# Windowed attention and a SoLU layer on one core: the layer's products five tiles apart, first tiles' h in halves over three PSUM banks, weights converted in contiguous staging, one batch's value means by TensorE

## The chip, the core and the metric

The kernel runs on one core of a Trainium2 chip. A core has five engines, each with its own queue of instructions: TensorE (PE, matrix products, with PEld for its weight loads), VectorE (DVE), ScalarE (ACT), GpSimd (POOL) and SyncE (SP, which here only issues transfers). An engine executes its queue in order, and waits at an instruction until the semaphores that it names have been raised by other engines or by transfers (DMA). The metric is the device time of one execution in microseconds; the time before is the median of three executions.

## What is computed

The reference, cut to what matters:

```python
def _attn_ref(q, k, v):                      # each (4, 8, 768, 64)
    block, window = (32, 16); nb = S // block; scale = 1 / sqrt(D)
    k_sum = k.reshape(B, H, nb, block, D).max(axis=3)
    v_sum = v.reshape(B, H, nb, block, D).mean(axis=3)
    scores_l = where(|i - j| < window, scale * q @ k.T, -1e9)
    scores_s = scale * einsum('bhsd,bhnd->bhsn', q, k_sum) + log(block)
    a = softmax(concatenate([scores_l, scores_s]))
    return a @ concatenate([v, v_sum])

def _moe_ref(x, w_in, w_out, g_ln):          # x (3072, 512), w_in (512, 1024), w_out (1024, 512)
    h = x @ w_in
    solu = h * softmax(h)
    ln = (solu - mean(solu)) / sqrt(var(solu) + 1e-6) * g_ln
    return ln @ w_out
```

The attention's output, laid out by tokens, is the layer's x. The weights arrive as 64-bit floats.

## The kernel before

**Tiles.** The layer runs over 24 tiles of 128 tokens (t = 0 to 23), six in each batch. Attention runs over groups of 256 queries, each in two halves of four heads; a half of a group is one step, and there are as many steps as tiles. A step has these parts, by the names in the trace: kw gathers the keys of each 64-query window (96 keys) and the 24 block maxima (ksum); s are the scores (L498, PE); e and nm the masked scores and their extremes (L518, VectorE, eight instructions); the exponentials (L526, ScalarE, eight); z their sums' reciprocals (L531, L532) and the scaling of e (L245 on VectorE or L246 on GpSimd); t the transposed e (L552, PE) and at its copy; x the values (L590, PE); xh and xl the high and low part of x in a reduced 32-bit format, of which products run in one pass.

**The layer.** `first(t)` makes h = x w_in with 24 products of 512 columns (L616: per 128 rows of w_in and half of h, low weights, low x, and both high). Then hm is h's maximum (L623), he the exponential (L625), hz its sum's reciprocal, he = h * he / z with the sum s1 (L629), he less its mean (L636 on GpSimd or L638 on VectorE), sq its squares (L641), y the reciprocal root (L646 to L652). `turn(t)` transposes he (lt, L552) and splits it into lh and ll. `second(t)` makes o with 24 products (L681), scales by y and stores. h holds two PSUM banks in one buffer, so `first(t + 1)` waits until L629 of tile t has read it.

**The main loop** (L724 to L759) records for tile t: values and scores of coming steps, `first(t)`, turns, two pieces of w_out's conversion, `second(t - LAG)` with LAG = 3 at L741, and for batch b + 1 the block maxima and means of v.

**Weights.** Each of 16 pieces (128 x 512) is loaded as 64-bit words into raw (L297) and converted in `rounded`: the high word is scaled (L315 or L317), the low word scaled and rounded (L321 or L323), both in place in raw, so that their elements stand two words apart; the high one is shifted to staging (L326), the low one gets the sign merged (L330), and GpSimd adds both (L334). Then the high half is copied (L238 or L239) and the low half subtracted (L245 or L246); for w_out L356 and L358 do so with g_ln.

**Means of v.** Batch 0's are four products with a selector on raw rows (`mean_values_first`, L400). Those of later batches are trees of GpSimd additions (`add_rows`, L418 and L422) with a small product at the end (`mean_values`, L433). They go to vsum, and `load_v2` copies them four times into each window's vt.

**What sets the order.** The kernel records operations with costs, buffers and dependencies in `Plan`; `issue()` then places them with its own model of time, choosing among engines where an operation names several (`alt`), and writes every engine's queue. An operation marked `port` counts VectorE's contention with GpSimd. `keep_up` inserts products of zeros (L766) where PE would be idle in the first 80 us of that model. Rings of buffers (`Plan.buf`) say which earlier tile must be done with a buffer.

Of the kernel before, what the change touches and what calls it, by code (L numbers as in the profile page):

```python
# [27 lines left out]
G = 4  # L28
# [9 lines left out]
LAG = 3  # L38
NHE = 4
NEAR = 4  # L40
# [3 lines left out]
LOADS = "kqkqkqkqwwwwwwwwrrrvQV"  # L44
# [4 lines left out]
class Buf:  # L49


    def __init__(self, make, prev=None):
        self.make, self.prev, self.tile = make, prev, None
        self.ops, self.writers, self.readers, self.gone = [], {}, {}, False
# [14 lines left out]
class Plan:  # L69
# [6 lines left out]
    RATE = 360.0  # L76
# [4 lines left out]
    DEAR = {"dve": 0.7, "act": 0.3}  # L81
    HELD = 1.1
    SYNC = 0.13

    def __init__(self):
        self.ops, self.rings, self.idle = [], {}, None

    def buf(self, pool, shape, dtype, tag, bufs, name):
        ring = self.rings.setdefault(tag, [])
        slot = f"{tag}_{len(ring) % bufs}"  # L90
        b = Buf(lambda: pool.tile(shape, dtype, tag=slot, bufs=1, name=name),
                ring[-bufs] if len(ring) >= bufs else None)
        ring.append(b)
        return b

    def op(self, engine, cost, fn, r=(), w=(), nbytes=0, after=(), alt=(), port=False):
# [16 lines left out]
        for b, part in w:  # L113
            of(b.writers, part)
            of(b.readers, part)
            if b.prev is not None:
                deps.update(b.prev.ops)
                b.prev.gone = True
# [11 lines left out]
    def issue(self):  # L130
        ready, free, dma = {}, {}, 0.0
# [9 lines left out]
        def enter(o, at):  # L141
            for e in o.can:
                ready.setdefault(e, []).append((at, o))
# [4 lines left out]
        def cost(e, o, t):  # L148
            held = min(max(free.get("pool", 0.0) - t, 0.0), self.HELD) if e == "dve" and o.port else 0.0
            return o.can[e][0] * (2 if e == "pe" and t < self.COLD else 1) + held  # L150
# [23 lines left out]
        for o in self.ops:  # L174
            if not o.left:
                enter(o, 0.0)
        order = []
        while len(order) < len(self.ops):
# [5 lines left out]
            o.end = free[e] = t + cost(e, o, t)  # L184
            if o.nbytes:
# [3 lines left out]
            for u in o.users:  # L189
                u.left -= 1  # L190
                if not u.left:
                    enter(u, max(d.end for d in u.deps) + self.SYNC)
# [9 lines left out]
    def keep_up(self, at, done):  # L202


        for tag in "hxs":
            b = next((b for b in self.rings[tag] if b.ops[0] not in done), None)
            if b and (b.prev is None or all(o in done and o.end + self.SYNC < at for o in b.prev.ops)):
# [6 lines left out]
def attn_then_solu(ctx: ExitStack, tc: tile.TileContext, q, k, v, vb, w_in, w_out, g_ln, out):  # L214
# [13 lines left out]
    LO_W = ((dve, 0.6), (pool, 1.4))  # L228
    MUL_E = ((pool, 1.8), (dve, 1.07))
# [62 lines left out]
    raw, stage, wi, wo = {}, {}, {}, {}  # L292
# [7 lines left out]
    def load_w_in(c, nh):  # L300
        load_w(c * 2 + nh, w_in[c * P:(c + 1) * P, nh * 512:(nh + 1) * 512])

    def load_w_out(f, after):
        load_w(2 * NKC + f, w_out[f * P:(f + 1) * P, :], after)

    def rounded(key, st, part):
# [3 lines left out]
        to = lambda: st.ap[:, part]  # L310
        high = lambda: x.ap.rearrange("p (n t) -> p n t", t=2)[:, :, 1]
        low = lambda: x.ap.rearrange("p (n t) -> p n t", t=2)[:, :, 0]
# [3 lines left out]
            out=high().bitcast(F32), in_=high().bitcast(F32), func=AF.Copy, scale=2.0 ** -112),  # L316
            w=[(x, 1)], alt=[(dve, 0.34, lambda: nc.vector.tensor_scalar(  # L317
                out=high().bitcast(F32), in0=high().bitcast(F32), scalar1=2.0 ** -112, scalar2=None,
# [3 lines left out]
            out=low(), in_=low().bitcast(U32), func=AF.Copy, scale=2.0 ** -29), w=[(x, 0)],  # L322
            alt=[(dve, 0.34, lambda: nc.vector.tensor_scalar(  # L323
                out=low(), in0=low().bitcast(U32), scalar1=2.0 ** -29, scalar2=None, op0=ALU.mult))], port=True)

        op(dve, 0.34, lambda: nc.vector.tensor_scalar(  # L326
            out=to(), in0=high(), scalar1=3, scalar2=None, op0=ALU.logical_shift_left),
            r=[(x, 1)], w=[(st, part)], port=True)
# [3 lines left out]
            r=[(x, 1)], w=[(x, 0)])  # L332

        op(pool, 1.46, lambda: nc.gpsimd.tensor_tensor(out=to(), in0=to(), in1=low(), op=ALU.add),  # L334
           r=[(x, 0)], w=[(st, part)])
        hl = plan.buf(const, [P, 2, 512], F32R, f"w{key}", 1, f"w{key}")
        return (lambda: to().bitcast(F32)), hl

    def split_w_in(c, nh):
        if nh == 0:  # L340
            stage["in", c] = plan.buf(sb, [P, 2, 512], I32, "he", NHE, f"cv_in{c}")
        st = stage["in", c]
        w, hl = rounded(c * 2 + nh, st, nh)
        wi[c, nh] = hl
        copy(COPY_W, lambda: hl.ap[:, 0], w, r=[(st, nh)], w=[(hl, 0)], port=True)
        tt(LO_W, ALU.subtract, lambda: hl.ap[:, 1], w, lambda: hl.ap[:, 0].bitcast(F32),
           r=[(st, nh), (hl, 0)], w=[(hl, 1)])

    def split_w_out(f):
        if f % 2 == 0:  # L350
            stage["out", f // 2] = plan.buf(sb, [P, 2, 512], I32, "vrow", 2, f"cv_out{f // 2}")
        st = stage["out", f // 2]
        w, hl = rounded(2 * NKC + f, st, f % 2)
        wo[f] = hl
        gs = g_sb[:, f:f + 1]
        op(act, 0.61, lambda: nc.scalar.activation(out=hl.ap[:, 0], in_=w(), func=AF.Copy, scale=gs),  # L356
           r=[(st, f % 2), g_b], w=[(hl, 0)])
        op(dve, 0.66, lambda: nc.vector.scalar_tensor_tensor(  # L358
            out=hl.ap[:, 1], in0=w(), scalar=gs, in1=hl.ap[:, 0].bitcast(F32),
            op0=ALU.mult, op1=ALU.subtract), r=[(st, f % 2), (hl, 0), g_b], w=[(hl, 1)])  # L360
# [5 lines left out]
    def load_keys(b, p, after=()):  # L366
# [4 lines left out]
        op(sp, 0.05, lambda: nc.sync.dma_start(out=x.ap[:, i], in_=k[b, p]), w=[(x, i)], nbytes=P * SP * 4,  # L371
# [12 lines left out]
    def load_v_rows(b, i):  # L384

        rows = v[b, HALO + 2 * P * i:HALO + 2 * P * (i + 1), :].rearrange("(c p) n -> p c n", p=P)
# [415 lines left out]
```

## Time and profile before

| | us |
|---|---|
| median of 3 runs (418.41 to 419.27) | 418.68 |
| the profiled execution | 419.72 |
| its span, first to last instruction | 417.9 |
| PE busy in the span | 396.2 |
| products of zeros (L766) in it | 23.4 |
| VectorE, ScalarE, GpSimd busy | 284.1, 243.6, 124.2 |

The profile shows one execution. A row of the order of time has start, duration, engine, line, operation, output<-input, shapes, a count where like instructions were merged, and in brackets how long the engine had been idle and what ended that. A row of a group has busy time, mean ns of one instruction, and idle time ahead of it. Starts of queued instructions can be closer than their durations, since one begins while the last one drains. TensorE's clock was granted at 0.992 on average, with 0.68 between 50 and 60 us.

### The profile page before, as it was taken

The page shows a single profiled execution, that of the slowest core. Times are in us where ns is not written, and L with a number is a line of the kernel's source. Part 1 is how long each engine was busy: PE and PEld are TensorE (multiplying, and loading weights), DVE is VectorE, ACT ScalarE, POOL GpSimd, SP SyncE. Part 2 cuts the span into 40 slices and gives each one's busy share as a digit, 9 for nine tenths or more (in the row PEclk, how much of TensorE's full clock was granted, in tenths as well). Part 3 has the DMA queues.
Part 4 walks back from the last instruction along what each step waited for, and adds up shares of the span by engine and source line. Part 5 has one row for each costly group of instructions (what it writes and reads, how often), then busy time and mean ns, then how long its engine had stood idle before and what let it go on. Part 6 is the DMA issues. An engine that isn't in the chain of part 4 may idle for free.

```text
span 417.9 us, 9489 instructions
## 1 busy us (share of the span) xinstructions
PE 396.2 (95%) x3667; PEld 299.3 (72%) x3667; DVE 284.1 (68%) x841; ACT 243.6 (58%) x710; POOL 124.2 (30%) x172
## 2 busy tenths in 40 slices
PE   7999598889899999999999999999999999999996
PEld 3437376567678777777877777777777777777876
DVE  4998899996877776736876764564676567453440
ACT  4967889737556745745763673675675566332231
POOL 4676546887851101108102110110110100111010
PEclk9999879999999999999999999999999999999999
DMA  8999996428337412126134220241230000000011
GB/s 268 410 256 263 327 245 164 127 78 197 91 117 200 130 49 80 52 88 153 55 100 124 77 78 27 76 102 40 77 95 29 25 6 23 27 25 2 25 50 52
DMA packets 22929, 46.03 MB, mean 110 GB/s; under 512 B 1860, under 2 KB 8260, under 8 KB 22884
## 3 DMA queue, kind: packets, MB, share of 16 engines
q1 hardware_dynamic: 18096, 36.97, 31.4%
q10 hardware_dynamic: 4788, 8.46, 6.2%
q8 instruction: 29, 0.48, 0.5%
q14 instruction: 16, 0.13, 0.1%
HBM read 36.97 MB, written 6.29 MB: 104 GB/s over the span
## 4 chain that ended last, share of the span: by engine, by line
PE 58%; DMA 16%; DVE 15%; ACT 5%; POOL 3%; issue 1%; SPq 0%; DVEq 0%
PE h L616 26%; PE o L681 22%; DMA kraw<-in_k 4%; DMA vt<-in_v 4%; DMA raw<-in_w_out 4%; DVE hm L623 3%; DVE e L518 3%; DVE he L629 3%; ACT he L625 3%; PE x L590 3%; PE lt L552 3%; DMA st_v<-in_vb 2%; PE t L552 2%; PE s L498 2%; POOL st_v L418 2%; DMA raw<-in_w_in 2%
## 5 line engine op out<-in xcount | busy, mean ns | idle before, releaser
L616 PE MATMUL h<-w,xh 128*128 128x512 f32 x384 | 141.1, 405 | 8.2 <-DVE he L629 6.9
L681 PE MATMUL o<-w,lh 128*128 128x512 f32 (+1 forms) x400 | 142.4, 394 | 0.1
L616 PEld LDWEIGHTS h<-w,xh 128*128 128x128 f32 x384 | 72.4, 189 | 31.8 <-issue 11.0
L681 PEld LDWEIGHTS o<-w,lh 128*128 128x128 f32 x400 | 74.1, 188 | 19.0 <-issue 2.9
L681 PE MATMUL o<-w,ll 128*128 128x512 f32 (+1 forms) x200 | 77.2, 386 | 0.5 <-DVE ll L666 0.5
L616 PE MATMUL h<-w,xl 128*128 128x512 f32 x192 | 75.7, 394 | 0.0
L526 ACT ACTIVATE e<-e,nm 128x120 f32<-128x120 f32 x192 | 73.0, 384 | 1.1 <-DVE nm L518 1.1
L636 POOL TENSOR_SCALAR he<-he,nmu 128x512 f32<-128x512 f32 x27 | 23.8, 883 | 99.5 <-DVE nmu L632 99.3
L625 ACT ACTIVATE he<-h,hm 128x1024 f32<-128x1024 f32 x24 | 26.7, 1114 | 42.9 <-DVE hm L623 42.8
L238 ACT COPY at<-t 120x512 f32<-120x512 f32 x45 | 24.2, 587 | 41.5 <-PE t L552 41.4
L681 PEld LDWEIGHTS o<-w,ll 128*128 128x128 f32 x200 | 37.6, 188 | 8.0 <-DVE ll L666 0.8
L518 DVE CUSTOM_DVE_ANT_0 e<-s,mask 128x120 f32<-128x120 f32 x192 | 40.5, 275 | 2.8 <-PE s L498 2.8
L616 PEld LDWEIGHTS h<-w,xl 128*128 128x128 f32 x192 | 36.3, 189 | 6.8
L623 DVE TENSOR_REDUCE hm<-h 128x1 f32<-128x1024 f32 x24 | 29.3, 1221 | 14.9 <-PE h L616 14.9
L240 POOL COPY kw<-ksum 128x192 f32<-128x192 f32 (+1 forms) x26 | 9.4, 363 | 100.6 <-PE s L498 79.9
L641 ACT ACTIVATE sq<-he 128x1024 bf16<-128x1024 f32 x24 | 25.4, 1057 | 22.6 <-POOL he L636 20.6
L239 DVE CAST lh<-lt 128x512 fp32r<-128x512 f32 x23 | 15.8, 687 | 32.4 <-PE lt L552 27.1
L666 DVE TENSOR_TENSOR ll<-lt,lh 128x512 fp32r<-128x512 f32 x48 | 31.8, 684 | 8.5 <-ACT lh L238 8.1
L418 POOL TENSOR_TENSOR st_v<-st_v 96x512 f32<-96x512 f32 (+3 forms) x42 | 33.9, 816 | 8.8 <-DMA st_v<-in_vb 6.3
L526 ACT ACTIVATION_READ_ACCUMULATOR e<-e,nm 128x1 f32 x192 | 36.3, 189 | 0.0
L590 PEld LDWEIGHTS x<-at,vt 120*64 120x64 f32 (+1 forms) x768 | 25.4, 141 | 10.4 <-issue 5.2
L629 DVE SCALAR_TENSOR_TENSOR he<-h,hz,he 128x1024 f32<-128x1024 f32 x24 | 30.7, 1278 | 0.2
(79 smaller groups left out, 525.3 us busy)
## 6 DMA issues: line engine op xcount, KB each, us to landing
vt<-in_v SPq DMA_DIRECT2D x12, 768.0 KB, 5.8
kraw<-in_k SPq DMA_DIRECT2D x16, 400.0 KB, 7.5
out<-os ACTq DMA_DIRECT2D x23, 256.0 KB, 2.0
qt<-in_q SPq DMA_DIRECT2D x11, 512.0 KB, 4.0
st_v<-in_vb SPq DMA_DIRECT2D x12, 384.0 KB, 3.7
raw<-in_w_in SPq DMA_DIRECT2D x8, 512.0 KB, 7.1
raw<-in_w_out SPq DMA_DIRECT2D x8, 512.0 KB, 12.0
vt<-vsum ACTq DMA_DIRECT2D x11, 192.0 KB
```

What stands on the lines that cost most here:

```text
L238: by = {act: lambda: nc.scalar.copy(out=to(), in_=of()), dve: lambda: nc.vector.tensor_copy(out=to(), in_=of()), pool: lambda: nc.gpsimd.t ...
L418: op(pool, 0.15 + w * 0.0021, lambda w=w, o=o: nc.gpsimd.tensor_tensor(out=o.ap[:n, :w], in0=x.ap[:n, :w], in1=x.ap[:n, w:2 * w], op=ALU.add),
L518: nc.vector.tensor_tensor_reduce(out=e.ap[:, n, :], in0=sc.ap[:, j, (2 * i + up) * KC:(2 * i + up + 1) * KC], in1=mask[:, mi, :], scale=-S ...
L526: nc.scalar.activation(out=e.ap[:, n, :], in_=e.ap[:, n, :], func=AF.Exp, bias=nm.ap[:, n:n + 1], scale=-1.0, accum_out=z.ap[:, n:n + 1])
L590: nc.tensor.matmul(xp.ap[j * D:(j + 1) * D, i, qs], vs.ap[:k, u, cs], at.ap[:k, u % 2, n[j] + u // 2, :], start=not apart, stop=not apart ...
L616: nc.tensor.matmul(o, a.ap[:, c, ts], w.ap[:, i], start=(c == 0 and n == 0), stop=(c == NKC - 1 and n == 2))
L623: op(dve, 1.13, lambda: nc.vector.tensor_reduce(out=nm.ap, in_=h.ap, op=ALU.max, axis=AX.X, negate=True), r=[h], w=[nm])
L625: op(act, 1.09, lambda: nc.scalar.activation(out=e.ap, in_=h.ap, func=AF.Exp, bias=nm.ap, accum_out=z.ap), r=[h, nm], w=[e, z])
L629: op(dve, 1.27, lambda: nc.vector.scalar_tensor_tensor(out=e.ap, in0=h.ap, scalar=z.ap, in1=e.ap, op0=ALU.mult, op1=ALU.mult, accum_out=s1 ...
L641: op(act, 1.13, lambda: nc.scalar.activation(out=sq.ap, in_=e.ap, func=AF.Square, accum_out=ss.ap), r=[e], w=[sq, ss])
L666: op(dve, 0.6, lambda part=part, r=r: nc.vector.tensor_tensor(out=part(lo), in0=tp.ap[:, r], in1=part(hi).bitcast(F32), op=ALU.subtract), ...
L681: nc.tensor.matmul(o.ap[:, cols], a.ap[:, f, :], w.ap[:, i, cols], start=(f == 0 and n == 0), stop=(f == NFC - 1 and n == 2))
```

## The change

In the order of the code:

- **LAG 5, NHE 6, NEAR 7.** `second(t)` is recorded five tiles behind `first(t)`; six buffers hold he; values and scores of a step are joined into one PE operation from tile 7 on, before from 4.
- **h in halves.** For tiles 0, 1 and 2 (EARLY = 3), the two halves of h are buffers of their own that go round over three banks, so that half of the next tile's h has a bank while the last is read; x and o then have one bank of four. From tile 3 on, h has banks 0 and 1 and x and o alternate between 2 and 3, as before. The early tiles have maximum, exponential and product of he in two instructions each, and one more to join maxima or sums.
- **Staging.** A piece's two words are converted straight to two contiguous halves of one staging buffer, one for each piece. The add may also run on VectorE: an instruction (printed as ISA) that adds 32-bit integers as 16-bit limbs.
- **Batch 1's means by TensorE** (`mean_values_pe`, MEANS = 2): raw rows vr, loaded in three pieces, four by four products with a selector in four row groups, a copy, and four small DMAs that bring 6 rows each into vsum. GpSimd's tree for that batch and its loads are gone; batches 2 and 3 keep theirs.
- **Layouts** made on the host: q by groups, k by pairs of heads, v as whole windows, batches 0 and 1 also as rows vr, so that a partition's words of a load are contiguous. First loads come as "kqkkqk", q in two loads of two head pairs.
- **The planner's numbers**: transfers at 400 instead of 360, a lower surcharge on VectorE, contention counted without a limit and also for GpSimd.

```diff
-LAG = 3
-NHE = 4
-NEAR = 4
+LAG = 5
+NHE = 6
+EARLY = 3
+MEANS = 2
+NEAR = 7
...
-LOADS = "kqkqkqkqwwwwwwwwrrrvQV"
+LOADS = "kqkkqkwwwwwwwwrrrvQV"
...
-    RATE = 360.0
+    RATE = 400.0
...
-    DEAR = {"dve": 0.7, "act": 0.3}
-    HELD = 1.1
+    DEAR = {"dve": 0.3, "act": 0.3}
...
+    ADD_W = ((dve, 0.62), (pool, 1.46))
...
-    def rounded(key, st, part):
+    def rounded(key, tag, bufs):
...
+        st = plan.buf(sb, [P, 2, 512], I32, tag, bufs, f"cv{key}")
+        words = lambda i: x.ap.rearrange("p (n t) -> p n t", t=2)[:, :, i]
+        high, low = (lambda: st.ap[:, 0]), (lambda: st.ap[:, 1])
...
-        op(pool, 1.46, lambda: nc.gpsimd.tensor_tensor(out=to(), in0=to(), in1=low(), op=ALU.add),
-           r=[(x, 0)], w=[(st, part)])
+        tt(ADD_W, ALU.add, high, high, low, r=[(st, 1)], w=[(st, 0)], port=True)
...
+    banks = ps.tile([P, 4, 512], F32, name="banks")
+    turn_x = [2]
+
+    def place_h(t, half):
+
+        if half is None:
+            return plan.place(lambda: banks[:, :2].rearrange("p i n -> p (i n)"), (0, 1), "h")
+        i = (2 * t + half) % 3
+        return plan.place(lambda: banks[:, i], (i,), "h")
+
+    def place_x(t):
+        i = 3 if t < EARLY else turn_x[0]
+        turn_x[0] = 5 - i
+        return plan.place(lambda: banks[:, i], (i,), "x")
...
+    def mean_values_pe(b):
+
+        vsum[b] = y = plan.buf(sb, [P, DM], F32, "vsum", 1, f"vsum{b}")
+        acc = plan.buf(ps, [P, 2, DM], F32, "s", 2, f"vs_ps{b}")
+        to = lambda: acc.ap[:, 0]
+
+        def mm(x, i, g, s):
+            nc.tensor.matmul(to()[g * 32:(g + 1) * 32], sel_q.ap[:, s, :], x.ap[:, i, :], start=s == 0, stop=s > 0)
...
+        rows = plan.buf(sb, [P, DM], F32, "os", 2, f"vs{b}")
+        op(act, 0.48, lambda: nc.scalar.copy(out=rows.ap, in_=to()), r=[acc], w=[rows])
+        for g in range(4):
+            op(act, 0.06, lambda g=g: nc.scalar.dma_start(
+                out=y.ap[WIN + 6 * g:WIN + 6 * g + 6, :], in_=rows.ap[32 * g:32 * g + 6, :]),
+               r=[rows], w=[(y, g)], nbytes=6 * 2048)
...
-        h = plan.buf(ps, [P, DF], F32, "h", 1, f"h{t}")
+        halves = t < EARLY
+        hs = [place_h(t, i) for i in range(2)] if halves else [place_h(t, None)]
```

The rows below are instructions in the order of one engine's queue, without times; the numbers behind names only tell buffers apart.

TensorE, behind tile 0's products, before: h_428 is tile 0, h_684 tile 1, s_1_1 the scores of the second step of group 1, t_1_0 the turn of its first.

```order
L616 MATMUL h_428<-w_533,xh_0_479 128x512
L616 MATMUL h_428<-w_533,xl_0_482 128x512
L616 MATMUL h_428<-w_533,xh_0_479 128x512
L498 MATMUL s_1_1_574<-kw_1_1_254,qt_1_132 64x120 x16
L766 LDWEIGHTS zero
...
L552 MATMUL t_1_0_638<-ident,e_1_0_522 120x64 x16
...
L616 MATMUL h_684<-w_284,xh_0_479 128x512
L616 MATMUL h_684<-w_284,xl_0_482 128x512
L616 MATMUL h_684<-w_284,xh_0_479 128x512
```

The same place now: banks is h in all rows, w_535 the last piece for tile 0, w_435 one for tile 1's first half.

```order
L666 MATMUL banks<-w_535,xh_0_456 128x512
L546 MATMUL s_1_1_568<-kw_1_1_234,qt_1_131 64x120 x16
L666 MATMUL banks<-w_435,xh_0_456 128x512
L666 MATMUL banks<-w_435,xl_0_459 128x512
L666 MATMUL banks<-w_435,xh_0_456 128x512
L844 LDWEIGHTS zero
...
L600 MATMUL t_1_0_660<-ident,e_1_0_540 120x64 x16
L844 LDWEIGHTS zero
L844 MATMUL banks<-zero 128x512
L666 MATMUL banks<-w_487,xh_0_456 128x512
```

The first half of tile 1's h now stands ahead of the turn t_1_0, among and behind tile 0's last products (w_268, w_358, w_376, w_435); the second half begins at w_487. Between s_1_1 and t_1_0 there are 12 products of zeros before and 16 now.

VectorE, in the middle of w_in's conversion, before: cv_in is staging, raw the words.

```order
L330 SCALAR_TENSOR_TENSOR raw_116<-raw_116 128x512
L326 TENSOR_SCALAR cv_in_378<-raw_120 128x512
L330 SCALAR_TENSOR_TENSOR raw_120<-raw_120 128x512
L326 TENSOR_SCALAR cv_in_251<-raw_110 128x512
L330 SCALAR_TENSOR_TENSOR raw_110<-raw_110 128x512
L326 TENSOR_SCALAR cv_in_271<-raw_114 128x512
```

The same place now: cv is staging, ISA the add, L257 with w the low half.

```order
L352 TENSOR_SCALAR cv_278<-cv_278 128x512
L348 SCALAR_TENSOR_TENSOR cv_282<-cv_282 128x512
L257 ISA cv_278<-cv_278 128x1024
L352 TENSOR_SCALAR cv_282<-cv_282 128x512
L348 SCALAR_TENSOR_TENSOR cv_339<-cv_339 128x512
L257 TENSOR_TENSOR w_376<-cv_278,w_376 128x512
L257 ISA cv_282<-cv_282 128x1024
```

GpSimd made all 16 adds before; now VectorE makes ten of them and GpSimd six. Of w_in's eight low halves GpSimd made four before and makes one now.

ScalarE, now, at batch 1's means: vs_ps are the products, vs their copy, at_2_0 the copies of the turned e for the next values.

```order
L579 ACTIVATE z_2_0_821<-z_2_0_821 128x8
L453 COPY vs_856<-vs_ps_816 128x512
L455 DMA vsum_863<-vs_856 6x512 x4
L511 DMA vt_0_807<-vsum_863 24x4x512
L250 COPY at_2_0_906<-t_2_0_886 120x512 x2
L681 ACTIVATE he_912,hz_913<-banks,hm_909 128x512 x2
```

The four small DMAs are new, and the one from vsum to vt, which waits for them, stands ahead of the copies. In later tiles, where the order repeats, TensorE's row from a step's scores to its turn holds 33 to 42 products of h and o before, mostly 36, and 30 now in most tiles, and from one tile's last product of h to the next tile's first stand 24 products of o, a turn of each kind, values and scores.

274 lines of the change are left out of this document (159 added, 115 removed).

## The prediction

> **What bounds the kernel now.** I read the page's busy shares and slices first, then the windows of three stretches, then TensorE's order of time.
>
> ```profile
> PE 396.2 (95%) x3667; PEld 299.3 (72%) x3667; DVE 284.1 (68%) x841; ACT 243.6 (58%) x710; POOL 124.2 (30%) x172
> DVE  4998899996877776736876764564676567453440
> 0.00:36.62 36.62, 32.83 (x297) 15.00 (x297) 31.11 (x65) 24.91 (x65) 23.45 (x36) 1.00 0.98 298
> 36.62:121.00 84.38, 72.85 (x702) 55.72 (x700) 72.77 (x206) 59.40 (x175) 57.16 (x70) 0.96 0.67 186
> 121.00:414.60 293.60, 290.44 (x2675) 228.59 (x2674) 180.26 (x571) 158.85 (x469) 43.62 (x68) 1.00 0.23 65
> ```
>
> The columns of a window are its length, then busy us of PE, PEld, DVE, ACT and POOL, PE's clock, DMA share and GB/s. From 121 us on TensorE is busy 290.4 of 293.6 us: its own work is the bound there, and only 3.2 us are open. All else lies ahead of 121 us. A busy PE isn't useful there, though, since line 766 fills waits with products of zeros:
>
> ```profile
> 0.00:36.62 36.62, 18.42 (x77) 7.46 (x77) 1.00 0.98 298
> 36.62:121.00 84.38, 4.97 (x34) 3.37 (x34) 0.96 0.67 186
> ```
>
> These rows are the same windows for line 766 alone. So before 36.6 us, where tile 0's first product starts, PE does 14.4 us of useful work (32.83 - 18.42), and in the next 84.4 us it idles 11.5 and fills 5.0. What ends its waits there:
>
> ```profile
> PE h L616 <- DVE he L629: 6.9, 7, 2.6
> PE t L552 <- POOL e L246: 5.1, 2, 4.8
> 43.84 1.48 PE L766 MATMUL x<-zero 128*128 128x256 bf16 x12
> 50.09 1.11 PE L552 MATMUL t<-ident,e 64*120 64x64 f32 x16 [4.77 <-POOL e L246]
> 52.65 0.76 PE L616 MATMUL h<-w,xh 128*128 128x512 f32 x1
> 68.36 0.47 PE L616 MATMUL h<-w,xh 128*128 128x512 f32 x1 [1.70 <-DVE he L629]
> 84.90 0.50 PE L616 MATMUL h<-w,xh 128*128 128x512 f32 x1 [2.63 <-DVE he L629]
> 109.41 0.47 PE L616 MATMUL h<-w,xh 128*128 128x512 f32 x1 [1.19 <-DVE he L629]
> ```
>
> h has one buffer: tile 1 starts at 52.65, 2 at 68.36, 3 at 84.90 and 5 at 109.41, each when VectorE has finished with the tile before. VectorE is the engine behind: nines over its slices from 10 to 41 us, and 72.8 of 84.4 us after 36.6. Part of that is waiting inside instructions:
>
> ```profile
> 22.10 0.68 DVE L330 SCALAR_TENSOR_TENSOR raw<-raw 128x512 int32<-128x512 int32 x1
> 22.71 0.41 DVE L326 TENSOR_SCALAR cv_in<-raw 128x512 int32<-128x512 int32 x1
> 23.04 1.78 DVE L330 SCALAR_TENSOR_TENSOR raw<-raw 128x512 int32<-128x512 int32 x1
> 35.10 0.68 DVE L245 TENSOR_TENSOR w<-cv_in,w 128x512 fp32r<-128x512 f32 x1
> 38.01 0.67 DVE L245 TENSOR_TENSOR w<-cv_in,w 128x512 fp32r<-128x512 f32 x1
> L334 POOL TENSOR_TENSOR cv_in<-cv_in,raw 128x512 int32<-128x512 int32 x8 | 11.8, 1477 | 4.2 <-DVE raw L330 4.2
> ```
>
> The columns of an instruction are start, duration, engine, line and operands. The same merge (L330) takes 0.68 us alone and 1.78 beside GpSimd's add (L334, 1.48 each): 1.1 us of contention each time. Starts run closer than durations: from the merge at 22.10 to the shift (L326) is 0.61, from there to the next merge 0.33.
>
> **The change, part by part.** I follow when h(t) can start. Prices:
>
> ```profile
> 97.56 5.87 PE h L616 x24
> 103.45 1.23 DVE hm L623
> 290.21 1.15 PE L590 MATMUL x<-at,vt 120*64 120x64 f32 x32
> 291.30 1.05 PE L498 MATMUL s<-kw,qt 64*64 64x120 f32 x32
> 292.28 0.50 PE L681 MATMUL o<-w,lh 128*128 128x512 f32 x1
> 287.51 0.69 PE L552 MATMUL t<-ident,e 64*120 64x64 f32 x16
> 288.03 0.66 PE L552 MATMUL lt<-ident,he 64*128 64x64 f32 x16
> 22.94 1.90 PE L400 MATMUL vs_ps<-st_v,sel 128*24 128x512 f32 x4
> 92.81 1.07 PE L433 MATMUL vs_ps<-vacc,ident 96*24 96x64 f32 x16
> ```
>
> By distances of starts: values (x) 1.1 us, scores (s) 1.0, a turn (t, lt) 0.6; a first product (24 matmuls) 5.87 with its pipeline's end, 5.7 to the next start; so 0.23 a matmul or filler and 0.7 for three; a mean product 1.90 per four. Half of a reduction of h (hm, 1.23) is 0.6.
>
> ```profile
> 7.58 0.95 DVE L380 TENSOR_REDUCE ksum<-kraw 128x24 f32<-128x768 f32 x1 [0.45 <-DMA kraw<-in_k]
> 8.45 0.27 DVE L518 CUSTOM_DVE_ANT_0 e<-s,mask 128x120 f32<-128x120 f32 x1
> 10.07 0.95 DVE L380 TENSOR_REDUCE ksum<-kraw 128x24 f32<-128x768 f32 x1
> 298.64 1.16 DVE L245 TENSOR_TENSOR e<-e,z 128x960 f32<-128x960 f32 x1
> 299.71 0.21 DVE L648 SCALAR_TENSOR_TENSOR y<-y,ss 128x1 f32<-128x1 f32 x1
> ```
>
> A score reduction is 1.6 (8.45 to 10.07), a scaling of e 1.07 (298.64 to 299.71).
>
> *To h(1)'s second half.* VectorE now does its four key maxima and both score reductions first and issues the conversion behind them as one run. The third keys landed by 7.58; the fourth, one load later, I put near 8.2: a maximum 0.95 and two reductions 3.2 end at 12.4. From there to the last low half that it makes, the order has 24 two-source operations of 512 words at 0.60, 15 one-source at 0.34, two scalings of e and two reciprocals at 0.1: 14.4 + 5.1 + 2.1 + 0.2 = 21.8 us. Waits add 2.6 by the same prices (z's reciprocal behind ScalarE's first conversion 1.1, a low half behind the copy of the means 0.9, the second half of x 0.6), two GpSimd adds left beside it 1.1 each, the new selector some 0.5: 39.5. That is no earlier than the last low half on VectorE now (begun at 38.01), but GpSimd is left with one low half where it has four. Then two score reductions 3.2, three half reductions of h 1.8, a merge and a shift 0.9, copying keys, e's scaling, reciprocals and the first half of he 2.6: 48. PE meanwhile does h(0) and half of h(1), which the third bank admits. So h(1) is half done when a bank comes free at **48**, against nothing of it at 52.65. Bounds: 45.3 without contention, 51 with the slow add below.
>
> *To h(3).* From 48 PE's order holds half of h(1) 2.8, three values 3.3, two turns 1.2, three scores 3.0, h(2) 5.7, the new mean products 3.8 (eight at 1.90 per four; GpSimd's tree for that batch goes, as do the old 1.1 us on PE) and 20 fillers 4.6: 24.4, so 72.4. ScalarE then issues four small DMAs and one that waits for them, all ahead of the copies of e (at) that the values need:
>
> ```profile
> 35.83 0.83 ACTq L462 DMA_DIRECT2D vt<-vsum  x1
> 36.70 0.62 ACT L238 CAST w<-cv_in 128x512 fp32r<-128x512 f32 x1 [0.36 <-issue]
> out<-os ACTq DMA_DIRECT2D x23, 256.0 KB, 2.0
> ```
>
> An issue holds ScalarE's queue 0.83 us, and a landing takes 2.0 on that queue: five issues and a landing are 6.2 us. By the same prices PE ends the means near 61.2 and could turn e by 65.5; their copy and the issues hold ScalarE to 68, so the copies of e come at 69 instead of 67: 2 us on the path, **74.4**. Bounds: 0 if values had to wait anyway, 4 if the small DMAs land later.
>
> *To h(4), h(5), h(6).* From the end of h(t) at 103.43 to h(t+1) at 109.41 the release takes 6.0 us now. h(4): 74.4 + 5.7 + 6.0 = 86.1, since only 4.7 us of PE's work lie between. With tiles five apart, 6.8 us of PE's work (turns, scores, values and 15 matmuls of o) lie between after that, so the release is covered: h(5) 98.6, h(6) **111.1**. Before, h(5) ended at 121.0 with 24 more o matmuls done (5.6) and a turn, a scores and a values fewer (2.7): the same state is reached at 121.0 - 5.6 + 2.7 = 118.1. Nominal gain 7.0.
>
> *What the count leaves out.* By these prices, the 84.4 us of before hold 63.2 us of work (six first products 34.2, 54 o matmuls 12.6, five t, s and x 13.5, three lt 1.8, means 1.1), but 67.9 (72.85 - 4.97) were busy: 4.7 more, of which about 2 are the slow clock (0.96 mean). I take half of the other 2.7 as lying on the path: 1.5. Gain 5.5. I leave the clock out of the new sum (0 to 2 us against).
>
> *Costs at nothing.* Batch 1's first loads are whole rows for each partition, and the windows hold 1 MB instead of 0.77. DMA moved 298 GB/s at 0.98 of its time in the first 36.6 us; faster transfers help only what waits for them, and the sum waits for VectorE. If they came 2 us later, 48 would move by up to 1. Two halves of h cost five more short VectorE instructions in each of three tiles (counted). After 111 us nothing is added; the tail's o products are the same.
>
> *The add on VectorE.*
>
> ```profile
> L629 DVE SCALAR_TENSOR_TENSOR he<-h,hz,he 128x1024 f32<-128x1024 f32 x24 | 30.7, 1278 | 0.2
> ```
>
> Ten of 16 adds move there as an instruction over 1024 16-bit elements; no row shows it. Bounds: 0.60, a 512-word operation of the same bytes, and 1.2, a two-source operation over 1024 elements (L629's mean is 1.28, its starts 1.2 apart). I take 0.60, by bytes.
>
> *Contiguous staging.* L330 reads and writes every second word and takes 0.68 alone; L245 takes 0.68 on neighbouring words. I count nothing. The Trainium skill ("Vector Engine (DVE) Microarchitecture Reference", section 5.2, Measured stream behaviour on trn2) has a port at full rate only over runs of two or more neighbouring words. By that rule the strided merge would be the slower one; these two rows disagree with it.
>
> **How the sum stands.** The profiled run took 419.72 us (span 417.9); the median is 418.68. Less 5.5: 414.2 on the profiled one, **413.2** as a median.
>
> **Rivals.**
> - *The add is slow (1.2).* Six adds before 48 us cost 3.6, of which the 2.6 us of waits hide 1.5; two stand ahead of h(4)'s release, 1.2. Gain 2.2: 416.5. For it: 1024 elements. Against: the bytes.
> - *Steady turns wait (slower).* From a tile's scores to its turn PE has mostly 36 matmuls now (8.4 us) but mostly 30 after (7.0).
>
> ```profile
> 297.12 1.06 ACT L641 ACTIVATE sq<-he 128x1024 bf16<-128x1024 f32 x1 [0.54 <-POOL he L636]
> ```
>
> Scores ended at 292.28 and e was ready at 299.71: 7.4 us. It decides from 7.0. At 0.5 us (with the wait's own 0.1) in some 14 tiles it costs 7.0: 420.2. Against: the square (1.06, and 0.54 idle ahead of it) stood between the exponentials and z; the new order has it ahead of the exponentials or behind z, which leaves about 5.9.
> - *Nothing comes of it.* What half a tile wins goes in PE's 46 fillers ahead of h(5), against 34 now, which are spent whether PE waits or not, and in VectorE's backlog, which moves to later tiles: 418.7. For it: VectorE stays at nine tenths to 48 us in my own sum.
> - *Neighbouring words are faster.* At best a merge then takes a one-source operation's 0.34: eight merges ahead of 48 us give 2.1, so 411.1. The skill's rule above is for it, the two rows against.
>
> **Chances.** Forecast 0.60 (409 to 416), slow add 0.17 (nearly all faster), steady wait 0.10, nothing 0.06, the rule 0.03, better for other reasons (no clock dip, a shorter landing) 0.04. The range 408.8 to 417.9 leaves out the slower case and most of "nothing". Faster by over 0.2% (what a measurement of this kernel can tell) 0.83, within 0.07, slower 0.10.
>
> **What would show it.** h(1)'s second half near 48, h(3) near 74, h(4) near 86, h(6) near 111; the add at 0.6 in VectorE's rows; ScalarE idle behind DMA issues near 62 to 68; no wait of t in steady tiles. Wrong if PE waits for VectorE past 90 us, or if t waits after 120.

## The result, and the profile after

| | us |
|---|---|
| the kernel before, median of 4 runs beside it (418.41 to 419.92) | 418.98 |
| the changed kernel, median of 4 runs (553.08 to 558.88) | 555.52 |
| ratio, 95% interval | 1.326 [1.318, 1.335] |
| span of the profiled run, before and after | 417.9, 555.5 |

It is slower by 136.5 us; the forecast was 413.2. Two of the twelve executions of e11 below fell in a slower state of the chip, and its ratio leaves them out. The page of the changed kernel, busy times and then TensorE's slices and clock:

```profile
PE 430.4 (77%) x3650; PEld 303.4 (55%) x3657; DVE 297.2 (54%) x899; ACT 226.6 (41%) x682; POOL 96.3 (17%) x152
PE   7987777698678777777777877867877777787876
PEclk8998978989799999999999999999999999899889
```

TensorE is busy for 77% of the span, where it was for 95%, and no engine has taken its place as the bound. Its slices are mostly sevens and eights to the end, so the loss lies in the steady tiles too, which the prediction had left as they were. The windows say the same (columns as in the prediction: length, busy us of PE, PEld, DVE, ACT, POOL, clock, DMA share, GB/s):

```profile
0.00:36.62 36.62, 31.43 (x276) 14.31 (x278) 27.59 (x72) 22.95 (x62) 13.74 (x37) 0.95 0.96 370
36.62:121.00 84.38, 65.18 (x558) 41.72 (x563) 55.07 (x175) 45.01 (x140) 16.63 (x17) 0.88 0.38 129
121.00:540.00 419.00, 323.13 (x2752) 238.27 (x2753) 213.62 (x651) 157.94 (x481) 65.90 (x99) 0.98 0.18 58
```

From 121 us on TensorE is open for 95.9 of 419 us, where it was open for 3.2 of 293.6. What it waits for, from the view of waits (who waited for whom, us in total, times, longest). After the change h is L666, o L755, x L639; L691 is the exponential of h, L698 the product he, L250 ScalarE's copies:

```profile
PE banks L755 <- ACT he L691: 26.4, 19, 1.4
PE banks L755 <- DVE he L698: 26.0, 18, 2.3
PE banks L666 <- ACT xh L250: 13.4, 15, 1.0
```

And one steady tile in order of time (in brackets the engine's idle time ahead of the row, and what ended it):

```profile
402.15 1.11 ACT L691 ACTIVATE he<-banks,hm 128x1024 f32<-128x1024 f32 x1 [5.00 <-DVE hm L689]
403.41 0.50 PE L755 MATMUL banks<-w,lh 128*128 128x512 f32 x1 [1.44 <-ACT he L691]
406.08 0.40 PE L755 MATMUL banks<-w,lh 128*128 128x512 f32 x1
406.51 1.28 DVE L698 SCALAR_TENSOR_TENSOR he<-banks,hz,he 128x1024 f32<-128x1024 f32 x1 [1.79 <-PE banks L755]
407.86 0.50 PE L755 MATMUL banks<-w,lh 128*128 128x512 f32 x1 [1.39 <-DVE he L698]
413.48 0.50 PE L666 MATMUL banks<-w,xh 128*128 128x512 f32 x1 [1.00 <-ACT xh L250]
```

These are waits between different banks. The o products of 403.41 write bank 2; the exponential that they wait for reads h in banks 0 and 1. At 406.51 VectorE, about to read banks 0 and 1, had waited 1.79 us for products of o in bank 2, and at 407.86 o waits in turn for VectorE. At 413.48 h, in bank 0, waits for ScalarE's copy of x from bank 3. No value passes between them. They share only the buffer: `banks`, one tile of four banks. The Trainium skill ("Perfetto Trace Analysis", section Matmuls) says that independent groups of products should rotate through different PSUM banks, so that emptying one overlaps the next group. This trace shows banks in rotation and waits all the same, 1.44 and 1.39 us in one tile's o alone: here the rotation alone did not bring that overlap.

### The profile page after: what moved, and what is told of

It reads as the page before. It is cut to its first block, busy times and chain, and to the rows that moved or that the text cites. A ratio compares the mean times of both kernels' runs of the same rounds, so it can differ in the third digit from the quotient of the medians.

```text
span 555.5 us, 9490 instructions
## 1 busy us (share of the span) xinstructions
PE 430.4 (77%) x3650; PEld 303.4 (55%) x3657; DVE 297.2 (54%) x899; ACT 226.6 (41%) x682; POOL 96.3 (17%) x152
## 5 line engine op out<-in xcount | busy, mean ns | idle before, releaser
L755 PE MATMUL banks<-w,lh 128*128 128x512 f32 (+1 forms) x400 | 140.6, 408 | 64.6 <-ACT he L691 26.4
L666 PE MATMUL banks<-w,xh 128*128 128x512 f32 x384 | 144.5, 429 | 37.3 <-ACT xh L250 13.4
L755 PEld LDWEIGHTS banks<-w,lh 128*128 128x128 f32 x400 | 76.0, 192 | 94.3 <-ACT he L691 31.6
L666 PEld LDWEIGHTS banks<-w,xh 128*128 128x128 f32 x384 | 75.7, 197 | 76.7 <-ACT xh L250 20.2
L755 PE MATMUL banks<-w,ll 128*128 128x512 f32 (+1 forms) x200 | 78.9, 395 | 1.4 <-DVE ll L740 1.4
L666 PE MATMUL banks<-w,xl 128*128 128x512 f32 x192 | 78.4, 409 | 0.0
L691 ACT ACTIVATE he<-banks,hm 128x1024 f32<-128x1024 f32 x21 | 23.4, 1115 | 86.1 <-DVE hm L689 78.2
L698 DVE SCALAR_TENSOR_TENSOR he<-banks,hz,he 128x1024 f32<-128x1024 f32 (+1 forms) x27 | 31.3, 1164 | 34.7 <-PE banks L755 25.8
L755 PEld LDWEIGHTS banks<-w,ll 128*128 128x128 f32 x200 | 38.6, 193 | 8.5 <-DVE ll L740 2.0
L666 PEld LDWEIGHTS banks<-w,xl 128*128 128x128 f32 x192 | 38.1, 198 | 6.3
L639 PEld LDWEIGHTS banks<-at,vt 120*64 120x64 f32 (+1 forms) x768 | 25.4, 141 | 13.2 <-issue 9.1
L639 PE MATMUL banks<-at,vt 120*64 120x64 f32 (+1 forms) x768 | 29.1, 229 | 3.5 <-DVE he L698 2.8
```

Source lines behind the costliest of these rows:

```text
L639: nc.tensor.matmul(xp()[j * D:(j + 1) * D, i, qs], vs.ap[:k, u, cs], at.ap[:k, u % 2, n[j] + u // 2, :], start=not apart, stop=not apart o ...
L666: nc.tensor.matmul(o, a.ap[:, c, ts], w.ap[:, i], start=(c == 0 and n == 0), stop=(c == NKC - 1 and n == 2))
L691: op(act, 1.2, lambda: nc.scalar.activation(out=e.ap, in_=hp.ap, func=AF.Exp, bias=nm.ap, accum_out=zs.ap[:, 0:1]), r=[hp, nm], w=[e, zs])
L698: op(dve, 0.67 if halves else 1.27, lambda i=i, hp=hp, part=part: nc.vector.scalar_tensor_tensor(out=part(), in0=hp.ap, scalar=zs.ap[:, 0: ...
L755: nc.tensor.matmul(o.ap[:, cols], a.ap[:, f, :], w.ap[:, i, cols], start=(f == 0 and n == 0), stop=(f == NFC - 1 and n == 2))
```

## The experiments

The theory was that waits are put by tile, not by bank, so that all that writes or reads h, x and o now goes in single file. Rival A: the new order, products five tiles apart, costs the time. Rival B: the banks themselves collide. "Three tiles" and "four tiles" in the runs' names are buffers in PSUM, not the 24 tiles of tokens. All runs, in the order of the text ("turns ahead" is explained below); the kernel before took 418.6 to 419.7 us beside them, on several chips, so that the ratios compare better than the times. Where an edit changes what the planner sees, it orders the engines anew, so that e3 and e4 beside e2, e8 and e11 to e14 beside e5, and e15 beside e14 differ in more than the edit names; the other pairs differ only where the text says:

| run | us | ratio to before, 95% interval |
|---|---|---|
| e1: before, with one tile | 560.75 | 1.336 [1.330, 1.343] |
| e2: after, three tiles | 420.78 | 1.002 [1.000, 1.005] |
| e3: after, four tiles, h in halves throughout | 422.19 | 1.007 [1.003, 1.010] |
| e4: e2 without early halves | 426.39 | 1.016 [1.012, 1.021] |
| e5: e2, turns ahead | 414.40 | 0.991 [0.988, 0.994] |
| e8: e3, turns ahead | 415.28 | 0.993 [0.989, 0.996] |
| e6: e5, second means' transfers by SyncE | 414.91 | 0.993 [0.989, 0.996] |
| e9: e5, s, t and lt in one-bank tiles | 413.59 | 0.991 [0.988, 0.994] |
| e10: e8, s, t and lt in one-bank tiles | 414.35 | 0.987 [0.983, 0.991] |
| e11: e5 without early halves | 423.43 | 1.006 [1.002, 1.010] |
| e14: e5, copies of means by SyncE | 411.79 | 0.985 [0.982, 0.988] |
| e15: e14 without early halves | 417.14 | 0.997 [0.994, 1.000] |
| e12: e5, add by GpSimd alone | 417.38 | 0.994 [0.991, 0.997] |
| e13: e5, four tiles apart | 412.53 | 0.983 [0.978, 0.987] |
| e16: e13, one-bank tiles as in e9 | 410.11 | 0.981 [0.978, 0.985] |

### One tile or several

```diff
+    banks = ps.tile([P, 4, 512], F32, name="banks")
+    plan.slots = {"h": [banks[:, :2]], "x": [banks[:, 2], banks[:, 3]]}
...
-        h = plan.buf(ps, [P, DF], F32, "h", 1, f"h{t}")
+        h = plan.view("h", 1, whole)
```

That is e1, in the kernel before (x, o and the first means likewise). e2, in the changed kernel:

```diff
-    banks = ps.tile([P, 4, 512], F32, name="banks")
+    h01 = ps.tile([P, 2, 512], F32, name="h01")
+    bank = [h01[:, 0], h01[:, 1], *(ps.tile([P, 512], F32, name=f"bank{i}") for i in (2, 3))]
...
-            return plan.place(lambda: banks[:, :2].rearrange("p i n -> p (i n)"), (0, 1), "h")
+            return plan.place(lambda: h01[:].rearrange("p i n -> p (i n)"), (0, 1), "h")
```

> The kernel before with one edit: h, x and o become views of one PSUM tile of four banks, as in the changed kernel, in place of a tile each. Every engine's instructions and their order stay those of the kernel before; only waits differ. Theory (the one tile): writers and readers of different banks of it now wait for each other, so the time goes from 419 us to 530 to 560, and steady tiles show products of o waiting for the readers of h. Rival A (the new order with products five tiles apart is what costs): nothing changes, 418 to 420. Rival B (the banks themselves collide, whichever tile they are in): x and o move from banks 6 and 7 to 2 and 3, beside h in 0 and 1; if that is what costs, the time goes up as well, but without more waits on semaphores between banks.

> The changed kernel with one edit: banks 0 and 1 are one tile, banks 2 and 3 a tile each; every engine's instructions, their order and the banks stay those of the changed kernel. Theory (the one tile): the waits between h, x and o go; what is left is the prediction's sum with some waits between the two halves of early h, which still share a tile: 411 to 420 us, TensorE busy over 9.8 of 10 us from 130 us on. Rivals A (new order) and B (banks collide): it stays near 555.

In both pairs every engine has the same instructions in the same order; only names and waits differ. The waits of the built programs that join two instructions on different banks of the h, x, o tiles can be counted: none before, 251 after, 279 in e1, 8 in e2 (its two halves of early h). e1 came out at 560.75 and e2 at 420.78, each just above its range. In e1 the view of waits names products of o (L692 there) behind readers of h (the first fence). In e2 those groups are gone; the second fence is its line of busy times:

```profile
PE banks L692 <- DVE he L640: 23.8, 19, 1.4
PE banks L692 <- ACT he L636: 15.7, 20, 1.9
```

```profile
PE 400.1 (95%) x3649; PEld 300.8 (72%) x3657; DVE 294.4 (70%) x899; ACT 226.8 (54%) x682; POOL 97.3 (23%) x152
```

TensorE is busy again, in a window of 100 us, most of them steady tiles, for 97.45:

```profile
300.00:400.00 100.00, 97.45 (x758) 76.95 (x756) 56.46 (x154) 36.16 (x101) 9.30 (x13) 0.98 0.07 24
```

So the cause is settled: the tile makes the waits, and they add a third to the time of either kernel (420.78 to 555.52 and 419.58 to 560.75). Both rivals fall: A by e1 (old order, slow) and e2 (new order, not slow), B by e2, whose banks are those of the changed kernel. TensorE's idle time went from 125.1 us (555.5 - 430.4) to 20.1; the other 30.3 us are longer busy time, at a mean clock of 0.963 against 0.984, which I don't split further.

e3 gives each bank a tile and reads h in halves in all 24 tiles; e4 is e2 with `EARLY = 0`:

```diff
+    bank = [ps.tile([P, 512], F32, name=f"bank{i}") for i in range(4)]
...
-        i = (2 * t + half) % 3
+        i = (2 * t + half) % 3 if t < EARLY else half
...
-        halves = t < EARLY
+        halves = True
```

> The changed kernel with a tile for each of the four banks, and with h of all 24 tiles read in halves (two maxima, exponentials and products instead of one, since no tile spans two banks now); the planner orders it anew. Theory (the one tile): no wait between banks is left, so the early tiles keep their halves' gain: 409 to 417 us, at or below the run with three tiles. Against it, the halves cost VectorE and ScalarE about 0.5 us each in each steady tile; if these are on the path, up to 10 us more: 420 to 426. Rivals A and B: near 555.

> The changed kernel with three tiles and without the early halves (EARLY = 0: h of all tiles whole in banks 0 and 1, x and o in turn in 2 and 3). By the prediction the halves brought tile 1 forward by some 4.6 us of the nominal 7.0; so by it this run is 3 to 5 us slower than the run with four tiles. If the halves bring nothing (their gain lies in products of zeros), it is within 1 us of the run with three tiles.

e3 missed the 409 to 417 of its theory: it is at 422.19, no better than e2, and inside the 420 to 426 for halves that cost on the path; e8 below tells which it is. e4 was 4.2 us slower than e3, inside the 3 to 5 that it gives to the halves, and 5.6 slower than e2; but its trace puts a loss elsewhere, which e14 and e15 take up. What remained was that e2 only equals the kernel before, where the prediction has it 5.5 us faster.

### The tail

At the end of e2 TensorE stops twice. Its order of time (lt are turns at L601, o is L756):

```profile
383.76 1.22 PE L601 MATMUL lt<-ident,he 64*128 64x64 f32 x32
386.33 0.49 PE L756 MATMUL bank<-w,lh 128*128 128x512 f32 x1 [1.35 <-DVE lh L251]
387.53 0.80 PE L756 MATMUL bank<-w,ll 128*128 128x512 f32 x1 [0.70 <-DVE ll L741]
388.12 1.05 PE L756 MATMUL bank<-w,lh 128*128 128x512 f32 x2
391.47 0.63 PE L756 MATMUL bank<-w,lh 128*128 128x512 f32 x2
```

And windows of 5 us, with the clock as the third number from the end:

```profile
385.00:390.00 5.00, 2.97 (x7) 2.18 (x8) 3.08 (x5) 1.53 (x3) 0.00 (x0) 0.75 0.15 56
390.00:395.00 5.00, 5.00 (x22) 3.98 (x21) 0.00 (x0) 0.29 (x1) 0.00 (x0) 0.91 0.00 0
405.00:410.00 5.00, 5.00 (x17) 3.94 (x16) 0.16 (x1) 0.00 (x0) 0.00 (x0) 0.71 0.00 0
```

With products five tiles apart, four turns are left when all h are done. They were recorded behind the o of the tile before and come in pairs (32 transposes in one row) in front of products that need them, with nothing else to do meanwhile: 2.05 us of waits, and then the clock is down, two products taking 1.05 us where they take 0.63 from 391.47 on. From 387.53 to 391.24 are nine products, 3.7 us in place of 2.1. The same follows at 400 us. In the kernel before, with products three tiles apart and two turns left, the tail's one wait was 0.49 us. e5 records each of the last turns one tile earlier:

```diff
-    second(NT - LAG)
-    for t in range(NT - LAG + 1, NT):
-        run(turn(t))
+    for t in range(NT - LAG, NT):
+        if t + 1 < NT:
+            run(turn(t + 1))
         second(t)
```

> The kernel with three tiles (420.8 us), and at the end each of the last turns is recorded ahead of the o products of the tile before, not behind them. Theory (the tail): with products five tiles apart four turns are left when all h are done; they stand in pairs in front of products that need them, and each pair costs a wait of about 2.1 us for lh and ll and then some 2 us at a lower granted clock (0.71 to 0.75 in two windows of 5 us). Both pairs gone gives 6 to 8 us: 413 to 415. Rival (the clock falls there by itself, for the run of dense products): only the waits go, 416 to 418. Rival (the early tiles are what keeps it from being faster than before): 420 to 421.

> The kernel with four tiles and h in halves throughout (422.2 us), with the last turns ahead of products as in the other run. Theory (the tail): 6 to 8 us less, 414 to 416. If steady halves cost on the path, it stays 1 to 2 us above the run with three tiles and turns ahead.

e5 has 414.40 and e8 415.28: 6.4 and 6.9 us less than without turns ahead by the medians, 4.7 and 5.8 by the ratios (the kernel before ran 1 us faster beside these two than beside e2 and e3). In e5 the turns stand singly, 6.4 us apart, and neither wait nor dip is left; two of its turns, and its window at the place of e2's dip:

```profile
380.15 0.71 PE L601 MATMUL lt<-ident,he 64*128 64x64 f32 x16
386.59 0.71 PE L601 MATMUL lt<-ident,he 64*128 64x64 f32 x16
```

```profile
385.00:390.00 5.00, 5.00 (x36) 3.85 (x35) 1.58 (x3) 1.27 (x2) 0.00 (x0) 1.00 0.15 55
```

The rival that the clock falls there by itself is out. e8 beside e5 also says that halves of h in all tiles, with a tile for each bank, cost nothing to be measured; e3's excess was the tail, and its place inside 420 to 426 was chance.

### ScalarE's queue, and tiles of the kernel before

e6 changes the queue of the second means' small transfers; e9 and e10 give s, t, lt and the sums of means two tiles of one bank instead of one of two:

```diff
-            op(act, 0.06, lambda g=g: nc.scalar.dma_start(
+            op(sp, 0.05, lambda g=g: nc.sync.dma_start(
```

```diff
-        tp = plan.buf(ps, [P, 2, NFC, QT], F32, "s", 2, f"lt{t}")
+        tp = plan.pair(ps, [P, NFC, QT], f"lt{t}")
```

> As the run with turns ahead, and the four small transfers of the second means are issued by SyncE's queue, not by ScalarE's. Theory (ScalarE held from 66.1 to 71.3 us by issues and a landing): the copies of e come up to 4 us earlier, but in that stretch TensorE waits only 0.8 us for them and fills 2 us with zeros, so 0 to 3 us less than the run with turns ahead. Rival (VectorE sets the pace up to 120 us): within 0.5 us of it.

> As the run with three tiles and turns ahead, and the tiles of two banks that hold s, t, lt and the sums of means become two tiles of one bank each; instructions and their order stay the same. This asks whether the rule of the one tile also cost the kernel before, which has the same tiles: here 116 waits between different banks go. Theory: copies of t and lt on VectorE and ScalarE no longer wait for each other, 0.6 us in each step before 120 us and 0.7 in each of the last turns; 1 to 3 us less than the run with turns ahead. Rival (TensorE is the bound after 130 us and VectorE before): within 0.5 us of it.

> As the run with four tiles and turns ahead (415.3 us), and s, t and lt in tiles of one bank too: no two banks share a tile any more, so no wait between banks is left. Theory: below both that run and the one with pairs of one-bank tiles (413.6): 411 to 414. Rival (TensorE and VectorE are busy there anyway): 413 to 416.

ScalarE is held as predicted, shown here by e2 in order of time: four issues in 2.89 us, a wait for their landing, a fifth issue, and only then the copy of e:

```profile
66.12 2.89 ACTq L456 DMA_DIRECT2D vsum<-vs  x4
70.40 0.84 ACTq L512 DMA_DIRECT2D vt<-vsum  x1
71.28 1.07 ACT L250 COPY at<-t 120x512 f32<-120x512 f32 x2 [5.19 <-DMA vsum<-vs]
```

Taking it away brought nothing (0.993 against 0.991). In e9, 116 of 124 waits between banks go, on tiles that the kernel before has too; it is not told apart from e5, nor e10 from e8. All 116 are waits of VectorE or ScalarE, none of TensorE, which is the bound; waits of this kind need not cost.

### What the halves, the add and the distance are worth

e11 and e15 set `EARLY = 0`; e12 sets `ADD_W = ((pool, 1.46),)`; e13 and e16 set `LAG = 4` and `NHE = 5`. e14 and e15 change the queue in `load_v2`:

```diff
-        return op(act, 0.06, lambda: nc.scalar.dma_start(
+        return op(sp, 0.05, lambda: nc.sync.dma_start(
```

> As the run with three tiles and turns ahead (414.4 us) without the early halves (EARLY = 0). By the prediction the halves are worth 4.6 us of its nominal gain: 418 to 420. By the traces of three tiles with and without halves, tile 6 starts at 115.3 and 114.1, so they are worth nothing by then: 413 to 416, unless ScalarE is again held by a transfer's issue near 123 us (a wait of 2.9 us of TensorE and 2 us of lower clock behind it): 417 to 420, and then the rows at 120 to 135 us show it.

> As the run with three tiles and turns ahead, and the transfers that copy the means into the windows are issued by SyncE, not by ScalarE. Theory (ScalarE held by these issues until a window has landed): TensorE's wait of 2.0 us at 127.9 and the lower clock behind it go, 2 to 4 us less than with turns ahead: ratio to before 0.982 to 0.987. Rival (SyncE's queue now holds later loads back): the same or slower, 0.990 to 1.000.

> As the run before this one, without the early halves. If the halves carry the gain that the prediction gave them, it is 3 to 5 us slower than the run with halves; if the loss without halves was the wait at 131 us alone, it is within 1.5 us of it.

e11 is slower than all its ranges (423.43). The loss at another place that its expectation speaks of is this one, shown by e4 in order of time:

```profile
114.76 0.38 SPq L506 DMA_DIRECT2D vt<-in_v  x1
123.28 0.82 ACTq L512 DMA_DIRECT2D vt<-vsum  x1
124.14 0.59 ACT L250 CAST lh<-lt 128x512 fp32r<-128x512 f32 x1 [4.05 <-issue]
129.88 0.79 PE L756 MATMUL bank<-w,lh 128*128 128x512 f32 x1 [2.86 <-ACT os L761]
```

ScalarE stands 4.05 us at the issue of a transfer that copies means into a window. Its queue is in order, so everything behind the issue is late, and what it does late then holds o by 2.86 us. The issue waits for the load of the same window, which was issued at 114.76: in e2, e4 and e5 alike the trace's last record of that load's landing is 0.07 us ahead of the issue (123.21 in e4). The kernel before has no such wait in its program: its load left the rows of the means alone. The change loads whole windows, and the copy has to come behind the load. So this wait is of the change's own making.

e5 has a wait of 2.01 us at the same place. Its ScalarE idled 2.6 us ahead of the same issue, but also waited 0.88 us for VectorE afterwards, so its trace alone doesn't say how much of the 2.01 is the issue's. e14 gives these transfers to SyncE: 0.985, the gain expected, and from 121 to 145 us the clock is at 1.00, where e5 has 0.93.

e15 is e14 without early halves and 5.35 us slower, 1.2%, with intervals that don't touch, a little past the 3 to 5. In order of time, the second half of h(1) and the start of h(6) in e14, and then the starts of h(1) and h(6) in e15:

```profile
50.34 0.47 PE L667 MATMUL h<-w,xh 128*128 128x512 f32 x1
115.09 0.50 PE L667 MATMUL h<-w,xh 128*128 128x512 f32 x1
```

```profile
54.53 0.50 PE L667 MATMUL h<-w,xh 128*128 128x512 f32 x1 [0.24 <-DVE he L699]
117.91 0.50 PE L667 MATMUL h<-w,xh 128*128 128x512 f32 x1
```

With halves, half of h(1) is done by the time that all of it begins without them, and tile 6 starts 2.8 us earlier; at tile 8 it is 4.6 (145.12 and 149.68). So the prediction's 4.6 for the halves (52.65 - 48) is met in size, but only 2.8 of it stands at tile 6, where the prediction's sum ends. The size goes with the planner's order too: in e4 tile 6 starts at 114.09, earlier than with halves in e2 (115.30), and e11 is 9.0 us slower than e5. What the halves are worth by themselves is not isolated.

> As the run with three tiles and turns ahead, and the integer add of the weights on GpSimd alone, as before the change. By the prediction the adds on VectorE at 0.60 each are what lets VectorE be done by 48 us, since each add on GpSimd takes 1.46 and slows a merge beside it by 1.1: the second half of h(1) comes 2 to 4 us later and the time is 1 to 4 us longer, 415.5 to 418.5. Rival (the staging or the order does it, not the add): within 0.7 us of 414.4.

> As the run with three tiles and turns ahead, with products four tiles apart and five buffers of he (LAG 4, NHE 5). If the distance itself is worth something (it covers the release of h before 121 us), it is 1 to 4 us slower, 415.5 to 418.5; if it is not, 413.5 to 415.3, with the tail one product group shorter.

> Products four tiles apart, three tiles for h, x and o, turns ahead, and s, t, lt in pairs of one-bank tiles; copies of means by ScalarE as in the change. If the gains add, it is the fastest: ratio to before 0.978 to 0.983. If TensorE is the bound in what is left, it is that of four tiles apart, 0.981 to 0.985.

e12's median lies in its range, 3 us above e5; its ratio, 0.994 against 0.991, doesn't tell the two apart. e13 is below both its ranges and faster than e5, with intervals apart: a distance of five was worth nothing here. Whether the distance itself costs, or the planner's other order, which in e13 has no wait behind ScalarE near 128 us, stays open. e16 is the fastest of all, 410.11 us, 1.9% less than before, though not told apart from e13.

## Why the prediction was wrong

**The step that failed** is the one that lets a product start "when a bank comes free". It took the bank as the unit of waiting, as the planner does. The program's waits went by the PSUM tile, and the change had put h, x and o into one. From that step followed "After 111 us nothing is added": 251 waits between banks were, and they lengthened the time by 32%. The prediction's own sign of error came true: PE waits for VectorE past 90 us (26.0 us in one group alone). None of its rivals was this one; the waits of the built program would have shown it without a run.

**That "the tail's o products are the same"** failed too, by 4.7 to 6.4 us. The o products are the same, but the turns in front of them no longer had other work beside them, and the slower clock behind each pause of some 2.1 us added 1.6 to it. With both mended, e5 stands at 414.40: the other terms sum to 3.7 us (by the ratio) or 4.2 (by the medians) where 5.5 were forecast. The larger windows, also counted at nothing, cost ScalarE its wait for their load, above. Two roundings of the sum are loose, 1.5 for half of 2.7, and 51 for 48 with six adds slower by 0.6; neither decides anything. The terms one by one, by the rows of e2, which has the order of the changed kernel without its waits:

```profile
51.10 0.47 PE L667 MATMUL h<-w,xh 128*128 128x512 f32 x1
77.86 0.50 PE L667 MATMUL h<-w,xh 128*128 128x512 f32 x1
89.40 0.50 PE L667 MATMUL h<-w,xh 128*128 128x512 f32 x1 [0.58 <-DVE he L699]
102.32 0.39 PE L667 MATMUL h<-w,xh 128*128 128x512 f32 x1
115.30 0.50 PE L667 MATMUL h<-w,xh 128*128 128x512 f32 x1
```

- *h(1)'s second half at 48:* 51.10, 3.1 late. VectorE began its last low half at 40.77 and went on to the next operation at 41.37, where the sum has 39.5: 1.9 of the 3.1 were lost by then.
- *h(3) at 74.4:* 77.86. Less the 3.1 it began with, 0.4 off, and partly by luck. The new mean products took 2.0 (61.78 to 62.78 and 64.37 to 65.36, by starts) where the sum has 3.8; four issues, a landing and an issue held ScalarE 5.2 us against 6.2; and TensorE waited 1.5 us for readers of h (0.85 at 52.89, 0.62 at 60.19) that the sum leaves out.
- *h(4), h(5), h(6) at 86.1, 98.6, 111.1:* 89.40, 102.32, 115.30; the steps of 11.5, 12.9 and 13.0 against 11.7, 12.5 and 12.5. So at tile 6 the gain is 118.1 - 115.3 = 2.8, not 7.0 less 1.5.
- *The add at 0.60:* right where VectorE is alone, wrong beside GpSimd. VectorE in e2:

```profile
33.67 1.81 DVE L257 CUSTOM_DVE_ANT_0 cv<-cv 128x1024 uint16<-128x1024 uint16 x1
38.29 0.68 DVE L348 SCALAR_TENSOR_TENSOR cv<-cv 128x512 int32<-128x512 int32 x1
38.89 0.68 DVE L257 CUSTOM_DVE_ANT_0 cv<-cv 128x1024 uint16<-128x1024 uint16 x1
39.49 0.42 DVE L352 TENSOR_SCALAR cv<-cv 128x512 int32<-128x512 int32 x1
```

From the add at 38.89 to the next start is 0.60, and eight of the ten adds took under 0.7 (one beside GpSimd 1.81, one 1.18), so the rival of the slow add (1.2) falls. The merge (L348), now on neighbouring words, takes 0.68 as it did on every second one: the rival of neighbouring words falls as well.

- *Steady turns wait (the slower rival):* hardly; after 121 us e2 waits three times for a t, 1.5 us in all, where the rival had 14 tiles and 7.0.
- *Nothing comes of it:* e2's ratio of 1.002 looks like this rival, but not its reason; with the tail mended, e5 is at 0.991.
- *The release is covered with tiles five apart:* it is, h(5) and h(6) start without a wait in e2. With four apart h(5) waits 1.54 us in e13, which is faster still.

## What to carry to other kernels

What a framework waits for goes by its own unit, here the tile in PSUM: give each bank that is meant to turn on its own a tile of its own, and when buffers are merged, count the waits that the built program has gained before asking what the schedule gains. When a distance between stages grows, read the end of the kernel again, where the distance has to be paid back without cover. Before an issue is put on a busy engine's queue, ask what it waits for, since all behind it waits as well.

## What the runs showed of the hardware

After some pauses TensorE went at about half its rate for a while. In e5:

```profile
127.86 0.50 PE L756 MATMUL bank<-w,lh 128*128 128x512 f32 x1 [2.01 <-ACT os L761]
128.43 0.99 PE L756 MATMUL bank<-w,lh 128*128 128x512 f32 x2
```

From the turn at 125.17 to 127.86 there were only 16 transposes and a wait of 2.01 us; then two products took 0.99 us, not 0.63. The pairs in e2's tail, 3.8 us with little but transposes, did the same. The waits of 1.0 to 1.44 us in each steady tile of the changed kernel did not; a window of its steady tiles has the clock at 1.00:

```profile
300.00:400.00 100.00, 76.94 (x701) 57.12 (x702) 51.24 (x169) 41.55 (x132) 9.39 (x15) 1.00 0.21 62
```

Length alone doesn't decide it. The kernel before stood idle for 2.63 us, longer than the wait in e5, and went on at the full rate:

```profile
84.90 0.50 PE L616 MATMUL h<-w,xh 128*128 128x512 f32 x1 [2.63 <-DVE he L629]
85.47 0.63 PE L616 MATMUL h<-w,xh 128*128 128x512 f32 x2
```

The Trainium skill ("TensorE: Matmul & The Clock Gate", section What's actually happening) tells of a free-running window of activity of about 3.4 us behind the clock, and of the lower rate after an idle window. The pause of 2.7 us in e5 is shorter than that, and like pauses came out differently here; a window whose phase is free would allow the second. No run here tests the window's length or its phase.

VectorE's add of 16-bit limbs took 1.81 us beside an add on GpSimd (33.65 to 34.92 in e2) and 0.68 alone: as much contention, 1.1 us, as the prediction's rows have for a merge.
